# An attention kernel that feeds a mixture-of-experts layer: its start and the order of its stages and expert blocks were rearranged

## The chip, the cores and the metric

The kernel runs on one core of one Trainium2 chip. The metric is the device time of one execution in microseconds (us). The 13 executions of the kernel before lie within 0.24% of each other. For each kernel one execution was also profiled; its span, from the first to the last instruction, is about 2 us shorter than the time.

Ratios are the mean time of one kernel's runs over the mean time of the runs of the kernel before from the same rounds on the same chip. They are therefore not quite the ratios of the medians that are quoted beside them.

The engines are TensorE (PE in the profile, and PEld for its weight loads), VectorE (DVE), ScalarE (ACT), GpSimd (POOL, which here issues most DMAs) and SyncE (SP).

## The reference

Attention works on 4 batches of 8 heads. Each head has 768 positions in 8 blocks of 96 and a width of 64. A small 8 by 8 matrix per head goes through five Sinkhorn rounds and mixes the key blocks and value blocks. The attention output is a 3072 by 512 matrix x, which then goes through 8 experts, weighted by gates that take another eight Sinkhorn-like rounds.

```python
def _attn_ref(q, k, v, sort_net):
    # ... cut: shapes ...
    P = sort_net
    for _ in range(5):
        P = P - np.max(P, axis=-1, keepdims=True)
        P = np.exp(P)
        P = P / (np.sum(P, axis=-1, keepdims=True) + 1e-09)
        P = P / (np.sum(P, axis=-2, keepdims=True) + 1e-09)
    k_sorted = np.einsum('bhij,bhjcd->bhicd', P, k_b).reshape(B, H, S, D)
    v_sorted = np.einsum('bhij,bhjcd->bhicd', P, v_b).reshape(B, H, S, D)
    # ... cut: inside each block of 96: softmax(scale * q k_sorted^T) v_sorted ...

def _moe_ref(x, w_gate, w1, w2):
    P = np.exp(x @ w_gate - (x @ w_gate).max())
    for _ in range(8):
        P /= P.sum(1, keepdims=True) + 1e-09
        P /= P.sum(0, keepdims=True) + 1e-09
        P *= N / E
    for e in range(E):
        h = np.maximum(x @ w1[e], 0.0)
        out += P[:, e:e + 1] * (h @ w2[e])
```

## The kernel before

The kernel takes the heads in 16 pairs. A pair m goes through three stages. The first stage multiplies keys and values with a matrix R, built from the Sinkhorn result, and turns the queries with transposing matmuls. The second stage computes the scores, their exponents, and the turned values. The third, called the output stage below, computes the denominators, takes their reciprocals as Exp(-Ln), multiplies the exponents with the values, and writes into xtT, which holds x.

An expert block is a piece of `x @ w1[e]`: four matmuls of 128 by 512. It can run once the x of its batches is there. While attention goes on, such blocks fill TensorE between the stages. Before the first of them a pair takes 4.14 us (27.75 to 31.89 us), in which ScalarE is busy for 4.08 us, and its three stages need TensorE for only 2.69 us (1.0 + 0.98 + 0.71 us, by spacings near 45 us). Eleven of the 48 (expert, column) combinations, 88 blocks, are done this way, up to the point where the second layer starts.

The start: 36 matmuls on zeros ("spins") keep TensorE busy during the Sinkhorn rounds (10.86 of the first 13.20 us).

```python
    w_ = bank([128, 512])
    for _ in range(36):
        nc.tensor.matmul(w_, wide[:, 0:128], wide, start=True, stop=True)

    rs = ones.tile([32, 8], F32)
    Prep = carve([128, 8, 8, 16], BF16, 88 * KB)[0:32]
    Pt = P.rearrange("p i j -> p j i")
    nc.vector.reduce_max(out=rs, in_=P, axis=AX.X)
    nc.vector.tensor_sub(P, P, mkap(rs, [rs.ap[0], rs.ap[1], [0, 8]]))
    for it in range(5):
        nc.scalar.activation(out=P, in_=P, func=AF.Exp)
        nc.vector.reduce_sum(out=rs, in_=P, axis=AX.X)
        nc.vector.reciprocal(out=rs, in_=rs)
        nc.vector.tensor_tensor(out=P, in0=P, in1=mkap(rs, [rs.ap[0], rs.ap[1], [0, 8]]),
                                op=ALU.mult)
        nc.vector.reduce_sum(out=rs, in_=Pt, axis=AX.X)
        nc.vector.reciprocal(out=rs, in_=rs)
        if it < 4:
            nc.vector.tensor_tensor(out=Pt, in0=Pt, in1=mkap(rs, [rs.ap[0], rs.ap[1], [0, 8]]),
                                    op=ALU.mult)
        else:
            nc.vector.tensor_tensor(out=Prep, in0=mkap(P, [P.ap[0], [8, 8], [1, 8], [0, 16]]),
                                    in1=mkap(rs, [rs.ap[0], [0, 8], [1, 8], [0, 16]]), op=ALU.mult)
    pbp = bank([128, 8, 32])
    for i in range(8):
        nc.tensor.matmul(pbp[:, i, :], Prep[:, i].rearrange("g j c -> g (j c)"),
                         ident[0:32, 0:32], start=True, stop=True)
    Pbig = carve([128, 8, 32], F32, 90 * KB)
    nc.vector.tensor_copy(Pbig, pbp)
```

The stages. The kernel takes 8 buffers (banks) from PSUM, the memory that its matmuls write to, and `bank` hands them out in turn.

```python
    def stage1(m):
        kb, vb, qb = qkv[m]
        R = Rt[m]
        for src, dic, nm in ((kb, KT, "KT"), (vb, VT, "VT")):
            dic[m] = atp_.tile([128, 8, 6, 16], BF16, name=nm)
            for kh2 in range(2):
                b_ = bank([128, 3, 128])
                for k3 in range(3):
                    for h2 in range(2):
                        nc.tensor.matmul(b_[64 * h2:64 * h2 + 64, k3, :], src[:, h2, 3 * kh2 + k3, :],
                                         R[:, h2].rearrange("p i c -> p (i c)"), start=True, stop=True)
                dst = dic[m][:, :, 3 * kh2:3 * kh2 + 3, :].rearrange("d i kk c -> d kk i c")
                b_ = b_.rearrange("d kk (i c) -> d kk i c", c=16)
                if kh2 == 0 or (nm == "KT" and m > 5):
                    nc.scalar.copy(dst, b_)
                else:
                    nc.vector.tensor_copy(dst, b_)
        b_ = bank([128, 6, 128], BF16)
        for kk in range(6):
            for h2 in range(2):
                nc.tensor.matmul(b_[64 * h2:64 * h2 + 64, kk, :], qb[:, h2, kk, :], ident,
                                 is_transpose=True, start=True, stop=True)
        QT[m] = atp_.tile([128, 6, 128], BF16, name="QT")
        nc.vector.tensor_copy(QT[m], b_)
        if m + 1 < NPAIR:
            build_r(m + 1)

    def stage2(m):
        ATT[m] = [atp_.tile([96, 2, 384], BF16, name=f"at{h2}") for h2 in range(2)]
        for half in range(2):
            bb = [bank([96, 4, 96]) for _ in range(2)]
            for i4 in range(4):
                i = half * 4 + i4
                for h2 in range(2):
                    hs = slice(64 * h2, 64 * h2 + 64)
                    nc.tensor.matmul(bb[h2][:, i4, :], KT[m][hs, i].rearrange("d kk c -> d (kk c)"),
                                     QT[m][hs, :, 16 * i:16 * i + 16], start=True, stop=True)
            for h2 in range(2):
                nc.scalar.activation(out=ATT[m][h2][:, half, :], in_=bb[h2].rearrange("k i q -> k (i q)"),
                                     func=AF.Exp, scale=scale)
        b_ = bank([96, 8, 128], BF16)
        for i in range(8):
            nc.tensor.matmul(b_[:, i, :], VT[m][:, i].rearrange("d kk c -> d (kk c)"), ident, is_transpose=True,
                             start=True, stop=True)
        VS[m] = vs_[m % 2]
        nc.vector.tensor_copy(VS[m], b_.rearrange("c i (h d) -> c i h d", d=64))

    def stage3(m):
        b, hpi = m // 4, m % 4
        xo = xtT[:, hpi, b].rearrange("d kk (i c) -> d i kk c", c=16)
        for half in range(2):
            den = bank([128, 384])
            for h2 in range(2):
                nc.tensor.matmul(den[64 * h2:64 * h2 + 64, :], ones64[0:96], ATT[m][h2][:, half, :],
                                 start=True, stop=True)
            rc = atp_.tile([128, 384], F32, name="rc")
            nc.scalar.activation(out=rc, in_=den, func=AF.Ln)
            nc.scalar.activation(out=rc, in_=rc, func=AF.Exp, scale=-1.0)
            b_ = bank([128, 4, 96])
            for i4 in range(4):
                for h2 in range(2):
                    nc.tensor.matmul(b_[64 * h2:64 * h2 + 64, i4, :], VS[m][:, half * 4 + i4, h2, :],
                                     ATT[m][h2][:, half, 96 * i4:96 * i4 + 96], start=True, stop=True)
            nc.vector.tensor_tensor(out=xo[:, 4 * half:4 * half + 4],
                                    in0=b_.rearrange("d i (kk c) -> d i kk c", c=16),
                                    in1=rc.rearrange("d (i kk c) -> d i kk c", i=4, c=16), op=ALU.mult)
```

The order of stages and blocks:

```python
    def fill(n, both=True):
        for _ in range(n):
            if state["h"] >= len(blocks):
                return
            e, c, fb = blocks[state["h"]]
            if last_batch[c] > state["done"]:
                if state["m"] < 2:
                    spin(1)
                return
            h_block(e, c, fb, both)
            state["h"] += 1
    # ... cut ...
    build_r(0)
    for m in range(NPAIR + 3):
        state["m"] = m
        if m < NPAIR:
            stage1(m)
        if m + 4 < NPAIR:
            load_pair(m + 4)
        if m == 0:
            load_w1(0)
        if m == 5:
            load_w1(1)
        fill(1)
        if 1 <= m <= NPAIR:
            stage2(m - 1)
        fill(1)
        if 2 <= m <= NPAIR + 1:
            stage3(m - 2)
        fill(1)
        if m >= 6 and m % 4 == 2:
            gate(m // 4 - 1)
        fill(1)
        if m >= 5 and m % 4 == 1:
            state["done"] = m // 4 - 1
        if m in (11, 16):
            x_sums((m - 11) // 5)
```

The softmax here doesn't subtract the row's maximum and nothing guards it: scores larger than these inputs give would overflow.

## Time and profile before

| What | Before |
|---|---|
| Time, median of 13 runs | 678.72 us (678.14 to 679.74) |
| Span of the profiled execution | 676.4 us |
| First expert block starts (timeline) | 37.18 us |
| Second layer starts, after the last of the 88 blocks (timeline) | 151.95 us |
| From there to the end | 524.45 us |

The page's first part gives busy times, and its fourth part the shares of the chain of waits, the path of work that ended last. These are the lines for TensorE and for the chain by engine.

```profile
PE 665.0 (98%) x6508; PEld 546.2 (81%) x6534; DVE 541.2 (80%) x766; ACT 338.9 (50%) x640; POOL 121.7 (18%) x163
...
PE 93%; ACT 2%; POOL 1%; DMA 1%; issue 1%; DVE 1%; POOLq 0%; ACTq 0%
```

TensorE is the bottleneck nearly everywhere. A change can then help in three ways only: it gives TensorE less to do, it lets TensorE's useful work start sooner, or it removes gaps between pieces of that work.

The next view cuts the span into stretches. The columns are the stretch, its length, and the busy time and number of instructions of PE, PEld, DVE, ACT and POOL, then the granted TensorE clock (1.00 is full speed), the DMA share and GB/s.

```profile
0.00:13.20 13.20, 10.86 (x36) 4.15 (x36) 8.76 (x38) 2.77 (x7) 11.19 (x21) 1.00 0.93 126
13.20:20.25 7.05, 5.52 (x111) 3.98 (x112) 5.02 (x11) 3.02 (x8) 5.51 (x9) 1.00 1.39 199
20.25:37.18 16.93, 14.97 (x357) 12.53 (x357) 13.27 (x28) 16.32 (x41) 9.30 (x13) 1.00 1.26 204
...
152.11:676.40 524.29, 520.50 (x4733) 463.09 (x4734) 434.79 (x534) 228.39 (x398) 81.72 (x103) 1.00 0.47 85
```

PE's 10.86 us in the first stretch are spins, not work. From 20.25 to 37.18 us ScalarE is busy 16.32 of 16.93 us, and PE's 14.97 us there are stretched: the end of a matmul is modelled, so a busy PE is not a full PE. The work in it is read from the spacing of matmuls where TensorE runs without waits.

That is the third view: the timeline of TensorE over one pair that runs with expert blocks. The columns are start, length, engine, line, operation, output and inputs, the tile of the array that is used (rows * columns), the moving operand, and how many instructions were merged.

```profile
57.07 0.53 PE L183 MATMUL bank<-R,kb 128*64 128x128 bf16 x12
57.43 0.50 PE L183 MATMUL bank<-R,vb 128*64 128x128 bf16 x12
57.77 0.50 PE L194 MATMUL bank<-ident,qb 128*64 128x128 bf16 x12
58.20 1.04 PE L265 MATMUL bank<-xtT,w1r 128*128 128x512 bf16 x3
59.17 0.56 PE L209 MATMUL bank<-QT,KT 64*96 64x96 bf16 x16
59.66 0.65 PE L216 MATMUL bank<-ident,VT 128*96 128x128 bf16 x8
60.14 1.03 PE L265 MATMUL bank<-xtT,w1r 128*128 128x512 bf16 x4
61.10 0.35 PE L227 MATMUL bank<-at,ones 96*64 96x384 bf16 x2
61.29 0.34 PE L235 MATMUL bank<-at,bigf 96*64 96x96 bf16 x8
61.46 0.33 PE L227 MATMUL bank<-at,ones 96*64 96x384 bf16 x2
61.62 0.34 PE L235 MATMUL bank<-at,bigf 96*64 96x96 bf16 x8
61.89 1.90 PE L265 MATMUL bank<-xtT,w1r 128*128 128x512 bf16 x7
63.72 0.53 PE L183 MATMUL bank<-R,kb 128*64 128x128 bf16 x12
```

One pair takes 63.72 - 57.07 = 6.65 us. (Where a block shows three or seven matmuls instead of four or eight, a record is missing; the spacing shows that it ran.) A block streams in 4 x 0.216 = 0.86 us (the 12 matmuls from 127.11 us on take 2.59 us), but the single block at 60.14 is followed only 0.96 us later. Such gaps of about 0.1 us stand at several places of this pair.

### The profile page before, as it was taken

To read this page: it belongs to the slowest core of one execution; us is meant where nothing else is said; L and a number is where in the kernel's file an instruction comes from. 1 tells how busy PE (TensorE), PEld (TensorE's weight loads), DVE (VectorE), ACT (ScalarE), POOL (GpSimd) and SP (SyncE) were. 2 spreads that over 40 slices of the span, in tenths; PEclk is the share of its full clock that TensorE was granted. 3 is DMA by queue.
4 is the path that set the end of the run, shared out by engine and by line. 5 is a ranking of instruction groups with operands and counts; after the bars stand their busy time and mean duration, and the time that the engine had idled before them with its cause. 6 is when DMAs were issued, how large, how long until landed. Compare 5 with 4: busy or idle time off the path is not lost.

```text
span 676.4 us, 15404 instructions
## 1 busy us (share of the span) xinstructions
PE 665.0 (98%) x6508; PEld 546.2 (81%) x6534; DVE 541.2 (80%) x766; ACT 338.9 (50%) x640; POOL 121.7 (18%) x163
## 2 busy tenths in 40 slices
PE   7899999999999999999999999999999999999997
PEld 3765565448788888888888888888888888888886
DVE  6767666789899888987888997787698998677776
ACT  2888887662323444444544444444444454445441
POOL 8543000000212120121122032022012012102201
PEclk9999999999999999999999999999999999999999
DMA  9998108032365729551355678154075045235336
GB/s 141 204 205 119 24 2 126 0 71 66 113 160 120 162 82 181 82 79 16 64 79 92 112 115 134 35 79 62 17 124 96 2 78 78 28 53 79 43 83 125
DMA packets 45940, 59.77 MB, mean 88 GB/s; under 512 B 3760, under 2 KB 31408, under 8 KB 45744
## 3 DMA queue, kind: packets, MB, share of 16 engines
q0 software_dynamic: 37840, 50.35, 46.1%
q1 hardware_dynamic: 7616, 8.05, 4.1%
q8 instruction: 51, 0.84, 0.5%
q10 hardware_dynamic: 416, 0.39, 0.2%
q14 instruction: 17, 0.14, 0.1%
HBM read 59.79 MB, written 25.21 MB: 126 GB/s over the span
## 4 chain that ended last, share of the span: by engine, by line
PE 93%; ACT 2%; POOL 1%; DMA 1%; issue 1%; DVE 1%; POOLq 0%; ACTq 0%
PE a L515 25%; PE a L437 19%; PE g L515 12%; PE bank L265 11%; PE g L437 9%; PE b L515 6%; PE b L437 5%; PE bank L183 1%; DMA qb<-in_q_dram 1%; ACT at L212 1%; PE a L468 1%; PE bank L216 1%; PE bank L209 1%; PE bank L227 1%; ACT rc L230 1%
## 5 line engine op out<-in xcount | busy, mean ns | idle before, releaser
L515 PEld LDWEIGHTS <-bigf 128*128 128x128 bf16 x1520 | 148.7, 98 | 18.3
L524 POOL DMA_DIRECT2D out_dram<-bigf x92 | 72.4, 903 | 421.4 <-DVE bigf L534 397.4
L437 PEld LDWEIGHTS <-bigf 128*128 128x128 bf16 x1248 | 122.1, 98 | 14.1
L515 PEld LDWEIGHTS <-hS 128*128 128x128 bf16 x1152 | 112.6, 98 | 14.0 <-DVE hS L491 0.2
L477 DVE TENSOR_TENSOR bigf<-bigf 128x2048 bf16<-128x2048 bf16 x96 | 115.3, 1217 | 0.0
L442 ACT COPY bigf<-a 128x512 f32<-128x512 f32 x72 | 42.3, 587 | 114.9 <-PE a L437 107.9
L415 DVE CUSTOM_DVE_ANT_0 bigf<-g,bigf 128x512 bf16<-128x512 f32 x72 | 49.6, 689 | 51.5 <-ACT bigf L451 51.4
L437 PE MATMUL g<-xtT,bigf 128*128 128x256 bf16 x576 | 86.4, 273 | 0.0
L265 PE MATMUL bank<-xtT,w1r 128*128 128x512 bf16 x330 | 82.3, 379 | 1.6 <-DVE xtT L237 0.3
L437 PEld LDWEIGHTS <-w1r 128*128 128x128 bf16 x768 | 75.1, 98 | 8.7
L459 ACT ACTIVATE bigf<-a 128x512 bf16<-128x512 f32 x72 | 43.0, 597 | 44.0 <-PE a L437 44.0
L415 DVE CUSTOM_DVE_ANT_0 bigf<-b,bigf 128x512 bf16<-128x512 f32 x72 | 49.4, 687 | 19.3 <-ACT bigf L442 19.3
L265 PEld LDWEIGHTS <-w1r 128*128 128x128 bf16 x352 | 31.9, 99 | 32.7 <-issue 0.3
L447 ACT COPY bigf<-g 128x512 f32<-128x512 f32 x72 | 42.3, 587 | 23.2 <-PE g L437 23.1
L515 PE MATMUL a<-bigf 128*128 128x256 bf16 x384 | 52.9, 273 | 0.0
L451 ACT COPY bigf<-a 128x512 f32<-128x512 f32 x72 | 42.5, 590 | 20.2 <-PE a L437 19.1
L515 PE MATMUL a<-w2T,hS 128*128 128x256 bf16 x384 | 52.1, 273 | 0.0
L515 PE MATMUL g<-w2T,hS 128*128 128x256 bf16 x384 | 52.1, 273 | 0.0
L515 PE MATMUL a<-w2r,bigf 128*128 128x256 bf16 x384 | 50.9, 273 | 0.0
L415 DVE CUSTOM_DVE_ANT_0 bigf<-a,bigf 128x512 bf16<-128x512 f32 x72 | 49.3, 684 | 0.5 <-PE a L437 0.5
L515 PE MATMUL a<-w2T,bigf 128*128 128x256 bf16 x368 | 49.5, 273 | 0.0
L271 ACT ACTIVATE bigf<-bank 128x512 bf16<-128x512 f32 x62 | 37.1, 598 | 18.2 <-PE bank L265 16.7
(130 smaller groups left out, 986.9 us busy)
## 6 DMA issues: line engine op xcount, KB each, us to landing
out_dram<-bigf POOLq DMA_DIRECT2D x92, 256.0 KB, 5.3
w1r<-in_moe_w_dram POOLq DMA_DIRECT2D x6, 1024.0 KB, 10.7
bigf<-gdr SPq DMA_DIRECT2D x24, 256.0 KB, 6.5
bigf<-in_moe_w_dram POOLq DMA_DIRECT2D x6, 1024.0 KB, 14.6
w2r<-in_moe_w_dram POOLq DMA_DIRECT2D x4, 1024.0 KB, 12.3
kb<-in_k_dram POOLq DMA_DIRECT2D x16, 192.0 KB, 7.4
vb<-in_v_dram POOLq DMA_DIRECT2D x16, 192.0 KB, 7.3
qb<-in_q_dram POOLq DMA_DIRECT2D x16, 192.0 KB, 7.3
```

The lines of the kernel that those rows point to most:

```text
L183: nc.tensor.matmul(b_[64 * h2:64 * h2 + 64, k3, :], src[:, h2, 3 * kh2 + k3, :], R[:, h2].rearrange("p i c -> p (i c)"), start=True, stop= ...
L265: nc.tensor.matmul(b_, w1t[e][:, kk, fb * 128:(fb + 1) * 128], xf[:, kk, c * 512:(c + 1) * 512], start=(kk == 0), stop=(kk == 3))
L271: nc.scalar.activation(out=hT[e, c][:, fb, :], in_=b_, func=AF.Relu)
L415: nc.vector._custom_dve(TENSOR_ADD_SAT, out=out, in0=a, in1=b, s0=3.4028234663852886e38, s1=0.0)
L437: nc.tensor.matmul(b_[:, i, :], A[:, kk, 128 * (2 * j + i):128 * (2 * j + i) + 128], Bm[:, kk, :], start=(first and i == 0 and kk == 0), s ...
L442: nc.scalar.copy(cP1, al)
L447: nc.scalar.copy(cP5, ga)
L451: nc.scalar.copy(cU2, al)
L459: nc.scalar.activation(out=h[:, 4 + 2 * j:6 + 2 * j, 0:256], in_=al, func=AF.Relu)
L477: nc.vector.tensor_tensor(out=h, in0=h, in1=mkap(g, [g.ap[0], [0, f1 - f0], [1, 512]]), op=ALU.mult)
L515: nc.tensor.matmul(b_[:, g, :], A[P_][i][:, j, 128 * g:128 * g + 128], Bm[P_][i][:, j, :], start=(first and i == 0 and g == 0 and j == 0), ...
L524: nc.gpsimd.dma_start(out=out[bb * S:(bb + 1) * S].rearrange("(p kk) d -> kk p d", kk=6)[kk], in_=o_[:, tt, :], accum_op=ALU.add if p else ...
```

## The change

The change has these intents:

1. Bring four pairs through all their stages before anything else, plus one first stage, and then start expert blocks.
2. Turn the queries of pairs 0 and 1 during the Sinkhorn rounds, and load them earlier.
3. Shorten the end of the Sinkhorn chain: split the last product over VectorE and ScalarE, and build the first R straight from PSUM.
4. In each pair, take Ln, Ln, Exp, Exp instead of Ln, Exp, Ln, Exp, keep the output product back until `x_out`, and share the copies anew.
5. From pair 4 on, run scores, blocks, output stage of the pair before, first stage of the next pair, blocks.

The core of the diff:

```diff
-    w_ = bank([128, 512])
-    for _ in range(36):
-        nc.tensor.matmul(w_, wide[:, 0:128], wide, start=True, stop=True)
-
+    def spin(n):
+        b_ = bank([128, 512])
+        for _ in range(n):
+            nc.tensor.matmul(b_, wide[:, 0:128], wide, start=True, stop=True)
+
+    KT, VT, QT, ATT, VS, Rt = {}, {}, {}, {}, {}, {}
+
+    def turn_q(m, eng):
+        qb = qkv[m][2]
+        b_ = bank([128, 6, 128], BF16)
+        for kk in range(6):
+            for h2 in range(2):
+                nc.tensor.matmul(b_[64 * h2:64 * h2 + 64, kk, :], qb[:, h2, kk, :], ident,
+                                 is_transpose=True, start=True, stop=True)
+        QT[m] = atp_.tile([128, 6, 128], BF16, name="QT")
+        if eng is None:
+            return b_
+        eng(QT[m], b_)
+
+    spin(14)
     rs = ones.tile([32, 8], F32)
     Prep = carve([128, 8, 8, 16], BF16, 88 * KB)[0:32]
     Pt = P.rearrange("p i j -> p j i")
@@ -138,6 +155,12 @@
     nc.vector.tensor_sub(P, P, mkap(rs, [rs.ap[0], rs.ap[1], [0, 8]]))
     for it in range(5):
         nc.scalar.activation(out=P, in_=P, func=AF.Exp)
+        if it == 3:
+            nc.scalar.copy(QT[0], turned)
+        if it in (2, 4):
+            turned = turn_q(it // 2 - 1, None)
+            if it == 2:
+                spin(10)
         nc.vector.reduce_sum(out=rs, in_=P, axis=AX.X)
         nc.vector.reciprocal(out=rs, in_=rs)
         nc.vector.tensor_tensor(out=P, in0=P, in1=mkap(rs, [rs.ap[0], rs.ap[1], [0, 8]]),
...
@@ -148,33 +171,41 @@
             nc.vector.tensor_tensor(out=Pt, in0=Pt, in1=mkap(rs, [rs.ap[0], rs.ap[1], [0, 8]]),
                                     op=ALU.mult)
         else:
-            nc.vector.tensor_tensor(out=Prep, in0=mkap(P, [P.ap[0], [8, 8], [1, 8], [0, 16]]),
-                                    in1=mkap(rs, [rs.ap[0], [0, 8], [1, 8], [0, 16]]), op=ALU.mult)
+            nc.vector.tensor_tensor(out=Pt[:, :, 4:8], in0=Pt[:, :, 4:8],
+                                    in1=mkap(rs, [rs.ap[0], rs.ap[1], [0, 4]]), op=ALU.mult)
+            nc.scalar.copy(Prep[:, 4:8], mkap(P, [P.ap[0], [8, 4], [1, 8], [0, 16]], off=32))
+            nc.scalar.copy(QT[1], turned)
+            nc.vector.tensor_tensor(out=Prep[:, 0:4], in0=mkap(P, [P.ap[0], [8, 4], [1, 8], [0, 16]]),
+                                    in1=mkap(rs, [rs.ap[0], [0, 4], [1, 8], [0, 16]]), op=ALU.mult)
     pbp = bank([128, 8, 32])
     for i in range(8):
         nc.tensor.matmul(pbp[:, i, :], Prep[:, i].rearrange("g j c -> g (j c)"),
                          ident[0:32, 0:32], start=True, stop=True)
-    Pbig = carve([128, 8, 32], F32, 90 * KB)
-    nc.vector.tensor_copy(Pbig, pbp)
-
-    KT, VT, QT, ATT, VS = {}, {}, {}, {}, {}
+    Pbig = carve([128, 8, 32], BF16, 90 * KB)
 
...
+    def build_r(m, src):
         R = Rt[m] = atp_.tile([128, 2, 8, 16], BF16, name="R")
         nc.vector.tensor_tensor(
             out=R,
-            in0=mkap(Pbig, [Pbig.ap[0], [1, 2], [32, 8], [0, 16]], off=2 * m),
+            in0=mkap(src, [src.ap[0], [1, 2], [32, 8], [0, 16]], off=2 * m),
             in1=mkap(mask, [mask.ap[0], [0, 2], [0, 8], [1, 16]]),
             op=ALU.mult)
 
...
-    def stage1(m):
+    def stage1(m, mid=None):
         kb, vb, qb = qkv[m]
         R = Rt[m]
-        for src, dic, nm in ((kb, KT, "KT"), (vb, VT, "VT")):
+        acts = () if m == 3 else (("KT", 0),) if m == 2 else (("KT", 0), ("VT", 0)) if m < 6 else (("KT", 0), ("KT", 1), ("VT", 0))
+        for src, dic, nm in ((kb, KT, "KT"), (qb, QT, "QT"), (vb, VT, "VT")):
+            if nm == "QT":
+                if m not in QT:
+                    turn_q(m, nc.vector.tensor_copy)
+                if mid:
+                    mid()
+                continue
             dic[m] = atp_.tile([128, 8, 6, 16], BF16, name=nm)
             for kh2 in range(2):
                 b_ = bank([128, 3, 128])
@@ -184,22 +215,15 @@
                                          R[:, h2].rearrange("p i c -> p (i c)"), start=True, stop=True)
                 dst = dic[m][:, :, 3 * kh2:3 * kh2 + 3, :].rearrange("d i kk c -> d kk i c")
                 b_ = b_.rearrange("d kk (i c) -> d kk i c", c=16)
-                if kh2 == 0 or (nm == "KT" and m > 5):
+                if (nm, kh2) in acts:
                     nc.scalar.copy(dst, b_)
                 else:
                     nc.vector.tensor_copy(dst, b_)
...
-        if m + 1 < NPAIR:
-            build_r(m + 1)
-
-    def stage2(m):
-        ATT[m] = [atp_.tile([96, 2, 384], BF16, name=f"at{h2}") for h2 in range(2)]
+        if m + 1 < NPAIR and m:
+            build_r(m + 1, Pbig)
+
+    def scores(m):
+        ATT[m] = at_[m % 3]
...
                                      func=AF.Exp, scale=scale)
+
+    def turn_v(m):
...
+    AV = {}
+
     def stage3(m):
-        b, hpi = m // 4, m % 4
-        xo = xtT[:, hpi, b].rearrange("d kk (i c) -> d i kk c", c=16)
+        rc = []
         for half in range(2):
             den = bank([128, 384])
             for h2 in range(2):
                 nc.tensor.matmul(den[64 * h2:64 * h2 + 64, :], ones64[0:96], ATT[m][h2][:, half, :],
                                  start=True, stop=True)
-            rc = atp_.tile([128, 384], F32, name="rc")
-            nc.scalar.activation(out=rc, in_=den, func=AF.Ln)
-            nc.scalar.activation(out=rc, in_=rc, func=AF.Exp, scale=-1.0)
+            rc.append(atp_.tile([128, 384], F32, name="rc", bufs=4))
+            nc.scalar.activation(out=rc[half], in_=den, func=AF.Ln)
+        AV[m] = []
+        for half in range(2):
+            nc.scalar.activation(out=rc[half], in_=rc[half], func=AF.Exp, scale=-1.0)
             b_ = bank([128, 4, 96])
             for i4 in range(4):
                 for h2 in range(2):
                     nc.tensor.matmul(b_[64 * h2:64 * h2 + 64, i4, :], VS[m][:, half * 4 + i4, h2, :],
                                      ATT[m][h2][:, half, 96 * i4:96 * i4 + 96], start=True, stop=True)
+            AV[m].append((b_, rc[half]))
+
+    def x_out(m):
+        b, hpi = m // 4, m % 4
+        xo = xtT[:, hpi, b].rearrange("d kk (i c) -> d i kk c", c=16)
+        for half in range(2):
+            b_, rc = AV[m][half]
...
     def fill(n, both=True):
         for _ in range(n):
             if state["h"] >= len(blocks):
                 return
             e, c, fb = blocks[state["h"]]
             if last_batch[c] > state["done"]:
-                if state["m"] < 2:
-                    spin(1)
                 return
             h_block(e, c, fb, both)
             state["h"] += 1
+
+    def fill_two():
+        bs = blocks[state["h"]:state["h"] + 2]
+        bk = []
+        for kks in (range(3), range(3, 4)):
+            for n, (e, c, fb) in enumerate(bs):
+                if kks[0] == 0:
+                    if fb == 0:
...
-    build_r(0)
-    for m in range(NPAIR + 3):
-        state["m"] = m
+    build_r(0, pbp)
+    nc.scalar.copy(Pbig, pbp)
+    build_r(1, Pbig)
+    load_w1(0)
+    stage1(0)
+    load_pair(4)
+    stage1(1)
+    load_pair(5)
+    load_w1(1)
+    scores(0)
+    turn_v(0)
+    stage1(2)
+    load_pair(6)
+    scores(1)
+    stage3(0)
+    turn_v(1)
+    stage1(3)
+    load_pair(7)
+    x_out(0)
+    scores(2)
+    turn_v(2)
+    stage3(1)
+    scores(3)
+    x_out(1)
+    turn_v(3)
+    stage3(2)
+    x_out(2)
+    stage3(3)
+    stage1(4, lambda: x_out(3))
+    load_pair(8)
+    state["done"] = 0
+    fill_two()
+    for m in range(4, NPAIR + 1):
         if m < NPAIR:
-            stage1(m)
-        if m + 4 < NPAIR:
-            load_pair(m + 4)
-        if m == 0:
-            load_w1(0)
-        if m == 5:
-            load_w1(1)
-        fill(1)
-        if 1 <= m <= NPAIR:
-            stage2(m - 1)
-        fill(1)
-        if 2 <= m <= NPAIR + 1:
-            stage3(m - 2)
-        fill(1)
-        if m >= 6 and m % 4 == 2:
+            scores(m)
+            turn_v(m)
+        fill(1 if m < 8 else 2)
+        if m > 4:
+            stage3(m - 1)
+            x_out(m - 1)
+            if m % 4 == 0:
+                state["done"] = m // 4 - 1
+        if m + 1 < NPAIR:
+            stage1(m + 1)
+        if m + 5 < NPAIR:
+            load_pair(m + 5)
+        if m == 8:
+            fill_two()
+        else:
+            fill(2)
+        if m % 4 == 0:
             gate(m // 4 - 1)
-        fill(1)
-        if m >= 5 and m % 4 == 1:
-            state["done"] = m // 4 - 1
-        if m in (11, 16):
-            x_sums((m - 11) // 5)
-
+        if m in (9, 14):
+            x_sums((m - 9) // 5)
```

## The prediction

> **What bounds the kernel now.** TensorE. The page's first part has PE busy 665.0 of 676.4 us, and the chain of waits is 93% PE. From 152.1 us on (view by stretches) PE is busy 520.5 of 524.3 us, in code that the change leaves alone. What is left is the start. Until the first expert block, at 37.18 us in the timeline, PE does useful work for about 13.7 us only: six first stages at 1.0 us, five score stages at 0.98 and four output stages at 0.71 (spacings read near 45 us). The other 23.5 us are spin matmuls (36 at first, 10.9 us) and waits: for the Sinkhorn chain until 13.2 us, then for copies. From 20.25 to 37.18 us ScalarE is busy 16.3 of 16.9 us, and pairs come every 4.14 us, which is ScalarE's work for one.
>
> **What the change does.**
> 1. Expert blocks start after four pairs plus one first stage, not after six first stages and five score stages. That is the main gain.
> 2. Queries 0 and 1 are turned during the Sinkhorn, in idle PE and ScalarE time; 12 of 36 spin matmuls go.
> 3. The last Sinkhorn product (1.21 us on VectorE) becomes a small multiply and two halves on two engines, and the first R is built straight from PSUM, without the 0.43 us copy in front. Estimate: first useful pair at 13.8 instead of 14.57 us.
> 4. Ln, Ln, Exp, Exp replaces Ln, Exp, Ln, Exp, where each Exp waited for its Ln; some copies move to VectorE. With R's operands in bf16 its 0.42 us may shrink: [...] this trace agrees (512 bf16 elements of the x sums take 0.42 us, as 256 fp32 elements of R do). [...] I count on little.
> 5. Later, three blocks for a pair until pair 8, then four: 50 instead of 52 blocks are done when attention ends. The total of useful matmuls is unchanged.
>
> **Sum.** I laid the new order out, each engine in order, bank by bank, with the trace's durations; the same for the old order gives 37.3 us for the first expert block (trace: 37.2). The new one gives 29.4 us, with 11.8 us of useful work before it: waste 17.6 against 23.5 us, gain 5.9. Some 1.5 us go back: waits of 0.2 to 0.6 us for QT copies and banks in pairs 4 to 12, where scores follow their copies closely. Net 4.4 us, all on the critical path, since everything behind only shifts.
>
> Predicted: 674.3 us, 8 in 10 between 672.3 and 676.8. Faster by over 2% 0.01, within 2% 0.98, slower by over 2% 0.01.
>
> **What would show it.** In the timeline, first kb matmul near 13.8 and first expert block near 29.4 us; last attention-phase block near 147.7 instead of 152.1; the rest (524 us) unchanged within 0.5; ScalarE over 90% busy from 20 to 29 us; short waits of score matmuls for QT.
>
> **What would make it wrong.** The array's clock: now the first spins are 0.43 us apart until 7.2 us, 0.21 after (timeline). [...] with fewer spins and pauses of 2.5 us the array may slow again [...]. Late query loads could hold the Sinkhorn's Exp behind a QT copy. An unforeseen bank wait in the four-pair start, or late expert weights, would cost more.

Four passages are cut from it where the marks stand: what this case's traces do not show about R in bf16 and about the clock, and an estimate of the clock's cost that does not say from which numbers it comes. The sum: 5.9 - 1.5 = 4.4 us, and 678.7 - 4.4 = 674.3 us.

## The result

The changed kernel takes 672.55 us (median of 7 runs, 671.84 to 673.51), against 678.72 us before. The ratio is 0.9907, with a 95% interval of 0.9896 to 0.9917. The change is a gain of 0.9%, clear of noise. All outputs are right.

| What (profiled execution) | Before | Predicted | After |
|---|---|---|---|
| Time, median | 678.72 | 674.3 (672.3 to 676.8) | 672.55 |
| First matmul on keys | 14.57 | 13.8 | 13.69 |
| First expert block | 37.18 | 29.4 | 30.43 |
| Second layer starts | 151.95 | 147.7 | 146.36 |
| From there to the end | 524.45 | 524 | 524.44 |
| Span | 676.4 | | 670.8 |

The page of the kernel after, its first and fourth part:

```profile
PE 658.9 (98%) x6491; PEld 545.1 (81%) x6514; DVE 539.1 (80%) x766; ACT 337.2 (50%) x642; POOL 121.7 (18%) x163
...
PE 95%; DVE 3%; issue 1%; DMA 0%; ACT 0%
```

TensorE is still the bottleneck. The shares hardly move, because a gap that goes away at 98% busy is a small part of a long span. The whole gain lies before the second layer: behind it the two kernels take the same 524.4 us.

The stretches of the kernel after:

```profile
13.20:20.25 7.05, 6.39 (x135) 5.45 (x137) 5.50 (x12) 5.44 (x14) 5.04 (x7) 0.76 1.32 205
20.25:30.00 9.75, 8.68 (x193) 6.76 (x192) 7.98 (x18) 9.46 (x25) 4.28 (x6) 1.00 1.24 205
```

ScalarE is now busy 9.46 of 9.75 us from 20.25 to 30.00 us, so the four-pair start is still paced by it, as forecast. The clock column of the stretch from 13.20 us shows 0.76, where it showed 1.00 before.

One pair with four blocks in the kernel after, in the timeline of TensorE:

```profile
61.68 0.56 PE L233 MATMUL bank<-QT,KT 64*96 64x96 bf16 x16
62.17 0.65 PE L242 MATMUL bank<-ident,VT 128*96 128x128 bf16 x8
62.65 1.89 PE L301 MATMUL bank<-xtT,w1r 128*128 128x512 bf16 x7
64.47 0.52 PE L254 MATMUL bank<-bigf,ones 96*64 96x384 bf16 x4
64.82 0.51 PE L264 MATMUL bank<-bigf 96*64 96x96 bf16 x16
65.16 0.50 PE L214 MATMUL bank<-R,kb 128*64 128x128 bf16 x12
65.50 0.50 PE L143 MATMUL bank<-ident,qb 128*64 128x128 bf16 x12
65.83 0.50 PE L214 MATMUL bank<-R,vb 128*64 128x128 bf16 x12
66.27 1.90 PE L301 MATMUL bank<-xtT,w1r 128*128 128x512 bf16 x7
68.10 0.56 PE L233 MATMUL bank<-QT,KT 64*96 64x96 bf16 x16
```

The pair takes 68.10 - 61.68 = 6.42 us for the same matmuls as the 6.65 us before.

So three questions are open. What does the slow clock cost? Why is a pair 0.22 us shorter, where the prediction expected waits and a loss? And how much do the order and the new start bring, each by itself?

### The profile page after: what moved, and what is told of

Its sections match the earlier page's. It is cut to its first block, busy times and chain, and to the rows that moved or that the text cites. A ratio compares the mean times of both kernels' runs of the same rounds, so it can differ in the third digit from the quotient of the medians.

```text
span 670.8 us, 15351 instructions
## 1 busy us (share of the span) xinstructions
PE 658.9 (98%) x6491; PEld 545.1 (81%) x6514; DVE 539.1 (80%) x766; ACT 337.2 (50%) x642; POOL 121.7 (18%) x163
## 4 chain that ended last, share of the span: by engine, by line
PE 95%; DVE 3%; issue 1%; DMA 0%; ACT 0%
PE a L592 25%; PE a L514 19%; PE g L592 12%; PE bank L301 10%; PE g L514 9%; PE b L592 6%; PE b L514 5%; PE bank L214 1%; PE bank L242 1%; PE bank L233 1%; PE a L545 1%; PE bank L254 1%; PE bank L264 1%; PE bank L143 1%; PE bank L281 0%
## 5 line engine op out<-in xcount | busy, mean ns | idle before, releaser
L301 PE MATMUL bank<-xtT,w1r 128*128 128x512 bf16 x318 | 77.1, 379 | 1.0
## 6 DMA issues: line engine op xcount, KB each, us to landing
bigf<-in_moe_w_dram POOLq DMA_DIRECT2D x6, 1024.0 KB, 14.7
```

The costliest lines, as they stand in the source:

```text
L301: nc.tensor.matmul(b_, w1t[e][:, kk, fb * 128:(fb + 1) * 128], xf[:, kk, c * 512:(c + 1) * 512], start=(kk == 0), stop=(kk == 3))
```

## The experiments

This table collects the profiled executions. "Clock" is the mean granted clock over the span. In the kernel after a mean of 0.997 comes from about 3.4 us at a granted clock of 0.50 (14.4 to 17.8 us; 0.5 x 3.4 / 670.8 = 0.0025), so the column must be looked at before two rows are compared.

| Run | Clock | First block | Second layer starts | Span | Ratio to before (95%) |
|---|---|---|---|---|---|
| before | 1.000 | 37.18 | 151.95 | 676.4 | 1 |
| after | 0.997 | 30.43 | 146.36 | 670.8 | 0.9907 (0.9896 to 0.9917) |
| e1_warm | 1.000 | 29.22 | 145.16 | 669.6 | 0.9896 (0.9881 to 0.9911) |
| e2_order | 1.000 | 30.77 | 146.71 | 671.2 | 0.9917 (0.9904 to 0.9929) |
| e3_start | 0.997 | 34.39 | 149.17 | 675.8 | 0.9984 (0.9971 to 0.9996) |
| e4_ln_exp | 0.997 | 30.88 | 149.72 | 674.2 | 0.9954 (0.9942 to 0.9967) |
| e5_before_runs | 0.997 | 37.25 | 151.89 | 676.4 | 0.9982 (0.9969 to 0.9994) |
| e6_split | 0.997 | 30.44 | 146.20 | 670.7 | 0.9912 (0.9898 to 0.9925) |
| e7_gate_early | 1.000 | 33.65 | 148.39 | 672.9 | 0.9952 (0.9939 to 0.9966) |
| e8_one_run | 1.000 | 29.40 | 146.21 | 670.7 | 0.9910 (0.9896 to 0.9923) |
| e9_adjacent | 0.997 | 36.98 | 150.25 | 674.8 | 0.9954 (0.9941 to 0.9967) |
| e10_no_spin | 0.995 | 38.17 | 153.50 | 680.4 | 1.0039 (1.0022 to 1.0056) |
| e11_hole | 1.000 | 29.12 | 145.04 | 669.5 | 0.9895 (0.9882 to 0.9908) |

### The clock: e1_warm and e10_no_spin

The first experiment adds six spins to the changed kernel, in the hole of TensorE behind the second turn of queries.

```diff
-            if it == 2:
-                spin(10)
+            spin(10 if it == 2 else 6)
```

> The changed kernel with six more spin matmuls after the second query turn (about 11.1 to 12.4 us). Theory A (clock): the granted clock fell to 0.50 from about 14.3 to 17.6 us because TensorE was nearly idle from 11.05 to 13.7 us; filling that hole keeps 1.00, stages of pairs 0 and 1 run at full rate, first expert block comes 0.6 to 1.2 us earlier (29.3 to 29.8 instead of 30.43) and the time is 671.4 to 672.0 us. Rival B: that stretch waits for copies on VectorE and ScalarE anyway, so the clock is 1.00 but the time stays at 672.5 within 0.3.

These are single microseconds of the kernel after, in the view by stretches:

```profile
15.00:16.00 1.00, 1.00 (x22) 0.90 (x18) 0.90 (x2) 0.62 (x2) 0.72 (x1) 0.50 1.31 201
17.00:18.00 1.00, 1.00 (x12) 0.87 (x14) 0.09 (x2) 1.00 (x4) 0.76 (x2) 0.60 1.47 206
```

And these are the same two microseconds with the six spins:

```profile
15.00:16.00 1.00, 1.00 (x34) 0.85 (x29) 1.00 (x3) 1.00 (x3) 0.60 (x1) 1.00 1.29 198
17.00:18.00 1.00, 1.00 (x40) 0.91 (x35) 0.83 (x3) 0.74 (x2) 0.96 (x2) 1.00 1.21 213
```

The clock holds 1.00, and TensorE issues 34 instead of 22 and 40 instead of 12 matmuls in these two microseconds. The first expert block comes at 29.22 instead of 30.43 us, and the second layer starts 1.20 us earlier. Theory A holds: the pairs at the start did lose to the clock. The time is 671.97 us (median). That the gain is 1.2 us between two profiled executions does not make it 1.2 us on average: of the eight executions of the kernel after, two had a mean clock of 1.000 and spans of 670.0 us, and six had 0.995 or 0.997 and 670.5 to 671.6 us. The four executions with the spins all had 1.000 and spans of 669.6 to 670.2 us. The two ratios overlap, so the gain in time is likely but not clear of noise. That the spins hold the clock is clearer: all 12 executions with them (e1_warm, e8_one_run, e11_hole) had 0.999 or 1.000, and of the 17 executions of the new start and new order without them (the kernel after, e4_ln_exp, e6_split) only three had.

The kernel before has the same lottery. Of the nine executions measured beside this experiment, three had a mean clock of 0.999 or 1.000 and spans of 676.2 to 676.3 us; six had 0.995 or 0.997 and 677.4 to 677.7 us. Compared at full clock the change takes off 676.3 - 670.0 = 6.3 us; at 0.997 it takes off 677.4 - 670.8 = 6.6 us. So the clock blurs both kernels by about 1 us, and it is not the cause of the difference between them.

What makes the clock fall is not shown. In the kernel after it is 0.50 for about 3.4 us, from 14.4 to 17.8 us. TensorE was not empty before that: in the 3.4 us from 10.90 to 14.30 us, just before the drop, it counts as busy for 1.32 us. Nor does this number alone decide: e2_order was busy for only 0.80 us from 11.20 to 14.60 us and kept 1.00.

The other experiment goes the other way. It removes from the kernel before the seven spins that stand between the stages of pairs 0 and 1.

```diff
             if last_batch[c] > state["done"]:
-                if state["m"] < 2:
-                    spin(1)
                 return
```

> The kernel before without the seven spin matmuls between the stages of pairs 0 and 1 (they are not in the changed kernel either). Theory L (they stood on the chain: 0.8 us of the first pairs): first expert block 0.6 to 1 us earlier than 37.18, time down by 0.5 to 0.8 us where the clock stays 1.00. Rival M (they filled waits, and without them the clock falls to 0.50 more often): no gain or a loss, more executions with mean clock 0.997.

The time is 681.72 us, 0.4% slower than before, and all six executions have a mean clock between 0.994 and 0.997. In the profiled one the clock is at 0.50 for longer:

```profile
15.00:16.00 1.00, 1.00 (x24) 0.50 1.33 204
...
20.00:21.00 1.00, 1.00 (x17) 0.50 1.16 218
```

(This is the same view with TensorE alone: busy time and count, clock, DMA share, GB/s.) The first expert block comes 1.0 us later than before. Rival M is right about the outcome: without these useless matmuls the kernel is slower. Its mechanism is shown only in part. The clock fell at about 14.3 us, before the first of the removed spins would have run (15.92 us in the kernel before), so their absence did not start the slow stretch; it can only have made it last, here to about 21 us. And of the 4.0 us of span lost, 2.5 us are lost behind the second layer's start, where 526.9 instead of 524.45 us are spent; that is the wait of the next section.

### The order and the start, each alone: e2_order, e3_start, e7_gate_early

The second experiment keeps the new order and takes the start back (R in bf16 and the earlier loads of queries stay). "Order" here takes in all of intents 1, 4 and 5, so the copies and the order of Ln and Exp too.

```diff
-    spin(14)
+    spin(36)
-        if it == 3:
-            nc.scalar.copy(QT[0], turned)
-        if it in (2, 4):
-            turned = turn_q(it // 2 - 1, None)
... (the last Sinkhorn product as before, in one piece on VectorE)
-    build_r(0, pbp)
-    nc.scalar.copy(Pbig, pbp)
+    nc.vector.tensor_copy(Pbig, pbp)
+    build_r(0, Pbig)
```

> The new order of stages and blocks, but with the start as before: 36 spins, last Sinkhorn product whole on VectorE, copy of P to SBUF on VectorE before the first R, queries 0 and 1 turned in their first stage. Theory C (order is the main gain): about 674 us (673.3 to 674.8), first expert block near 31 us, so about 4.5 of the 6.2 us stay. Theory D (the early start is the main gain): 676 us or more.

It takes 673.19 us, ratio 0.9917. The order by itself brings most of the gain; theory C holds, and the value is at the better end of its range. Against e1_warm, which has the same order and also a full clock, the old start costs 30.77 - 29.22 = 1.55 us at the first block and 1.6 us of span. So the new start is worth 1.6 us in the new order when the clock holds, and 0.4 us in the profiled execution of the kernel after, where the clock fell.

The third experiment puts the new start into the old order of stages and blocks.

```diff
-    stage1(0)
-    load_pair(4)
... (the new sequence up to the end of the new loop)
+    for m in range(NPAIR + 3):
+        if m < NPAIR:
+            stage1(m)
... (the loop of the kernel before; stage2 is scores and turn_v, the output stage is followed by x_out;
     old copies, old order of Ln and Exp, no spins between the pairs)
```

> The new start (early query turns, split last product, first R from PSUM, bf16 R, no spins between pairs) in the old order of stages and blocks, old copies, old Ln and Exp order. Laid out with the durations of the trace: first expert block near 34 instead of 37.2 us and 675.5 us in all (674.8 to 676.5). Theory C strictly (only the order counts): 678 us, 0.8 us gained. If the clock falls as in the changed kernel, up to 1 us more.

The first block comes at 34.39 us and the second layer starts at 149.17 us, 2.8 us before the old one, although the clock fell to one half from about 13.0 to 16.4 us. But the time is 678.17 us, ratio 0.9984. The layout for this run was right up to the second layer, and the time was not. The span behind it is 526.6 instead of 524.45 us. The waits of TensorE from 140 us to the end name the place (columns: who waited for whom, us in total, times, longest):

```profile
PE a L564 <- DVE hS L540: 1.5, 1, 1.5
```

And the waits of VectorE between 100 and 160 us show what it waited for:

```profile
DVE bigf L526 <- DMA bigf<-gdr: 2.5, 1, 2.5
```

The final gates are written to DRAM and read back, spread over all partitions, before VectorE can multiply the experts' h with them and form the sums hS for the second layer. In the kernel before VectorE is busy with other sums from 142.93 to 147.81 us and goes on to this product at 147.85 us without a wait. The timelines show the issue of the first read and of the next expert's weights, and the start of VectorE's multiplication; first the kernel before, then e3_start:

```profile
144.54 0.90 SPq L403 DMA_DIRECT2D bigf<-gdr  x2
145.51 0.75 POOL L112 DMA_DIRECT2D w1r<-in_moe_w_dram  x1 [43.10 <-PE bank L265]
147.85 4.63 DVE L477 TENSOR_TENSOR bigf<-bigf 128x2048 bf16<-128x2048 bf16 x4
```

```profile
142.74 0.75 POOL L113 DMA_DIRECT2D w1r<-in_moe_w_dram  x1 [43.12 <-PE bank L299]
142.79 0.90 SPq L452 DMA_DIRECT2D bigf<-gdr  x2
147.59 3.50 DVE L526 TENSOR_TENSOR bigf<-bigf 128x2048 bf16<-128x2048 bf16 x3 [2.53 <-DMA bigf<-gdr]
```

In e3_start the 1 MB of weights was issued 0.05 us ahead of the gates, and VectorE starts at 147.59 us, 4.8 us after the read's issue. In the kernel before the gates went first, and VectorE starts without a wait 3.3 us after the issue. No run changed the order of these two DMAs alone, so that the weights slow the gates is not proven; but all 13 traces line up with it. In the eleven in which the read (256 KB) was issued 0.97 to 1.71 us ahead of the weights, VectorE started 3.2 to 3.7 us after the read's issue (in two of them, the kernel before and e5_before_runs, it waited for nothing, so the data may have landed sooner). In the two in which it came behind them it took longer: 4.8 us in e3_start, and 5.5 us in e10_no_spin, where it came 0.23 us behind. The weights' place explains only part of the wait in e3_start: there the read was issued 2.6 us after the write of the gates, against 1.6 us in the kernel before, and no run shows why. The kernel after has this wait of VectorE too (1.6 us), but it has 13 instead of 11 blocks left after the gate rounds, and TensorE does not notice (none of its waits from 140 us on names hS).

The seventh experiment tests that. It is e3_start with two blocks moved from pair step 16 to behind attention, so that the last gate stands 1.7 us earlier against the blocks. (With that the read of the gates also comes 1.1 us ahead of the weights, so both things change at once.)

```diff
             x_out(m - 2)
-        fill(1)
+        if m != 16:
+            fill(1)
         if m >= 6 and m % 4 == 2:
             gate(m // 4 - 1)
-        fill(1)
+        if m != 16:
+            fill(1)
```

> The earlier run of the new start in the old order, with two expert blocks moved from pair step 16 to behind attention, so that the last gate comes 1.7 us earlier against the blocks (13 blocks left after the gate iterations instead of 11, as in the changed kernel). Theory I (the new start alone gained 2.8 us by the phase's end, and the gates' round trip through DRAM gave most of it back): the wait of the second layer for VectorE sums (1.5 us) is gone and the time is 1 to 2 us less than that run, 676 to 677. Rival J (the loss of that run is not this wait): the same 678 within 0.4.

It takes 675.63 us, ratio 0.9952. TensorE no longer waits for hS, and 672.9 - 148.39 = 524.5 us are spent behind the start of the second layer. At a mean clock of 0.996 or 0.997 its executions have spans of 673.5 to 673.9 us, against 675.4 to 676.6 us for e3_start. Theory I holds: the new start alone is worth about 3.3 us, and without these two blocks it gives two thirds of that back.

The order alone is worth 5.6 us and the start alone 3.3 us (0.83% and 0.48% of 678.7 us). Together they bring 6.3 us, not 8.9. They overlap, because both shorten the stretch before the first expert block: in the profiled executions at full clock it comes 6.4 us earlier with the order alone (e2_order), 3.5 us with the start alone (e7_gate_early) and 8.0 us with both (e1_warm).

### The 0.22 us of a pair: e5_before_runs, e6_split, e8_one_run, e9_adjacent

The first guess was that each run of expert blocks between other matmuls costs a gap. Three experiments change the number of runs. The fifth merges blocks in the kernel before, with the changed kernel's order inside the output stage:

```diff
-        fill(1)
+        fill(2 if m > 5 else 1)
         if 1 <= m <= NPAIR:
             stage2(m - 1)
-        fill(1)
+        if m < 6:
+            fill(1)
... (output stage: den, den, av, av and Ln, Ln, Exp, Exp)
```

> The kernel before with only the order inside a pair changed: from pair 6 on its four expert blocks stand in two runs instead of three, and the output stage goes den, den, av, av with Ln, Ln, Exp, Exp. Theory G (each change between blocks and attention matmuls costs TensorE about 0.1 us): the distance of pairs falls from 6.64 to about 6.42 us, phase end 2 to 3 us earlier, time 675.6 to 677 us if the gates' round trip does not take some of it back. Rival H (the 0.22 us came from the order of pairs and lost waits, not from switches): 6.6 us and 678 us or more.

The sixth parts the two blocks of the changed kernel in pairs 9 to 15:

```diff
             scores(m)
+            if m > 8:
+                fill(1)
             turn_v(m)
-        fill(1 if m < 8 else 2)
+        fill(2 if m in (8, 16) else 1)
```

> The changed kernel with the two blocks before the output stage parted, one ahead of the value turn, one behind it, in pairs 9 to 15: one more switch each way in seven pairs, no copy waited for sooner. Theory G: the distance of those pairs grows from 6.42 to 6.5 to 6.62 us and the time by 0.6 to 1.4 us, to about 673.5. Rival H: nothing changes within 0.3 us.

The eighth puts all four blocks of a pair into one run, on top of e1_warm:

```diff
-        fill(1 if m < 8 else 2)
+        fill(1 if m < 8 else 2 if m == 8 else 0)
...
-            fill(2)
+            fill(2 if m < 8 else 4)
```

> The changed kernel with the six spins of the first experiment and all four blocks of pairs 9 to 15 in one run. Theory G: another 0.1 us per pair, 0.7 us in all, and the QT wait near 72 us gone: 671.0 to 671.5. Rival: waits for exponents and banks, since output and first stage now follow the scores at once: 672 or more.

Theory G fell in all three. With fewer runs in the old order a pair still takes 63.54 - 56.89 = 6.65 us. (The time is 677.47 us, ratio 0.9982; four of its five executions had a full clock and spans of 675.2 to 675.7 us, so about 0.8 us were gained, most likely in the early pairs, which come every 3.84 instead of 4.14 us near 30 us; none of it comes from the later distance.) With one more run in the new order a pair takes 71.54 - 65.15 = 6.39 us, a little less than 6.42, and the time is the same (672.76 us). With one run the time is 672.73 us, 0.8 us more than e1_warm, and a pair takes 75.62 - 68.92 = 6.70 us.

The timelines hold the answer: the gaps stand where the column with the asterisk, the tile of the array, changes its kind. Here is a part of e5_before_runs:

```profile
60.34 0.65 PE L216 MATMUL bank<-ident,VT 128*96 128x128 bf16 x8
60.92 0.52 PE L228 MATMUL bank<-at,ones 96*64 96x384 bf16 x4
61.27 0.51 PE L237 MATMUL bank<-at,bigf 96*64 96x96 bf16 x16
61.71 1.90 PE L269 MATMUL bank<-xtT,w1r 128*128 128x512 bf16 x8
63.54 0.53 PE L183 MATMUL bank<-R,kb 128*64 128x128 bf16 x12
```

The value turn (128*96) takes 0.48 us where a block follows it, as at 62.17 us of the kernel after, and 0.58 us here, where the output stage (96*64) follows. The output stage takes 0.34 us for its second half where the first stage (128*64) follows, as at 64.82 us of the kernel after, and 0.44 us here, where a block (128*128) follows. Between two tiles of the same width of 64 columns there is no gap (the 0.34 us above), nor between a value turn and a block (the 0.48 us). Going by the tiles, a pair passes six changes in the old order: 64 columns (first stage), full (block), 64 rows (scores), full (turn, block), 64 columns (output), full (block), and again 64 columns. In the new order output stage and next first stage stand side by side, and four changes remain. Merging or parting blocks, as e5_before_runs and e6_split do, changes neither count, and neither does e8_one_run. Of its 0.28 us more, 0.17 us stand at the key matmuls (68.92 to 69.43 us: 0.51 instead of 0.34 us); where the rest comes from was not tracked down.

So the guess is now that a change of the tile's kind (theory K below calls it the tile mode) is what costs the time. The ninth experiment puts this to the test in the old order of pairs: from pair 6 on the output stage moves next to the following first stage, and its blocks stand ahead of it.

```diff
         fill(1)
+        fill(1 if m > 5 else 0)
         if 1 <= m <= NPAIR:
             stage2(m - 1)
         fill(1)
-        if 2 <= m <= NPAIR + 1:
-            stage3(m - 2)
-        fill(1)
         if m >= 6 and m % 4 == 2:
             gate(m // 4 - 1)
-        fill(1)
+        fill(1 if m > 5 else 0)
+        if 2 <= m <= NPAIR + 1:
+            stage3(m - 2)
+        fill(0 if m > 5 else 2)
... (output stage: den, den, av, av and Ln, Ln, Exp, Exp, as in e5_before_runs)
```

> The kernel before with den, den, av, av and, from pair 6 on, the output stage directly ahead of the next first stage (its block moved ahead of it; three runs of blocks became two). Theory K (what costs about 0.1 us is a change of tile mode of the array: full, 64 columns or 64 rows; the old order has six such changes a pair, the earlier run with merged runs still had six and gained nothing, the changed kernel has four): four changes, distance of pairs 6.42 to 6.45 us, phase end 1.5 to 2.3 us before 151.95. Rival H (the 0.22 us came from lost waits that only the new order of pairs removes): 6.6 us or more. The time itself may hide part of it where the gates' round trip binds: 676 to 677.5 us.

A pair now takes 61.70 - 55.28 = 6.42 us:

```profile
55.28 0.52 PE L228 MATMUL bank<-at,ones 96*64 96x384 bf16 x4
55.63 0.51 PE L237 MATMUL bank<-at,bigf 96*64 96x96 bf16 x16
55.97 0.50 PE L183 MATMUL bank<-R,kb 128*64 128x128 bf16 x12
...
61.70 0.52 PE L228 MATMUL bank<-at,ones 96*64 96x384 bf16 x4
```

The second layer starts at 150.25 us and the time is 675.81 us, ratio 0.9954. The same kernel order with six changes (e5_before_runs) has 0.9982. Theory K holds: two changes of the tile's kind fewer go with 0.22 us less for each pair (6.65 to 6.42 us), an estimate of about 0.11 us each, and this needs neither the new order of pairs nor the new start. What the change from the 64-row scores to a full-array matmul costs cannot be read here: such a matmul follows them in every order, and they take 0.49 us. The groups of weight loads show it from another side. These are the loads ahead of the key matmuls from 37 to 118 us (after the bar: idle time of the loader just before them, and what ended it). First the kernel before:

```profile
L183 PEld LDWEIGHTS <-kb 128*64 128x64 bf16 x108 | 3.3, 109 | 3.8 <-issue 3.8
```

Then the kernel after:

```profile
L214 PEld LDWEIGHTS <-kb 128*64 128x64 bf16 x120 | 3.8, 110 | 0.0
```

Before, the weight loader sat idle 0.42 us ahead of each of the nine groups of key matmuls in that stretch (9 x 0.42 = 3.8 us), and the first weights of the new kind were loaded only when their matmuls began (both at 63.72 us). After, the kind does not change there, and it does not sit idle; e9_adjacent, in the old order of pairs, shows 0.0 there too.

### The order of Ln and Exp: e4_ln_exp

The fourth experiment takes back Ln, Ln, Exp, Exp in the changed kernel.

```diff
         for half in range(2):
             den = bank([128, 384])
... (two matmuls)
             nc.scalar.activation(out=rc, in_=den, func=AF.Ln)
-        for half in range(2):
             nc.scalar.activation(out=rc, in_=rc, func=AF.Exp, scale=-1.0)
             b_ = bank([128, 4, 96])
... (the output matmuls)
```

> The changed kernel with Ln, Exp, Ln, Exp for a pair again, and den, av, den, av on TensorE. Theory E (the pairing matters because the output product of a pair stands ahead of the next pair's query copy on VectorE): waits of about 0.5 us at blocks or scores in most pairs, 675 to 676 us. Rival F (ScalarE is off the critical path after the start, [...]): 673 to 674 us.

(From rival F a clause is cut, a cost of tile changes for each pair that no run shows; it was the author's reason for 0.5 to 1.5 us over the 672.55 us of the changed kernel.)

It takes 676.09 us, ratio 0.9954: 3.5 us are lost, half of the gain. The size is theory E's, but its mechanism is not. The waits of TensorE from 13.2 us on name a copy of queries only once, for 0.3 us before the first block; in the pairs they name the Ln:

```profile
PE bank L299 <- ACT rc L257: 1.5, 7, 0.2
PE bank L214 <- ACT rc L257: 0.8, 2, 0.6
```

The second Ln stands behind the first Exp on ScalarE, which itself waits for the first Ln, so the second bank of denominators comes free later, and the block (L299) or the next key matmul (L214) that is to use this bank waits. The pairs with four blocks take 6.7 us, for example 79.67 - 72.94 = 6.73 us. In most of them a wait of 0.21 us for the Ln makes up most of the 0.26 us by which they are longer (6.68 instead of 6.42 us); the rest was not tracked down. In the old order the same change of Ln and Exp left the pair at 6.65 us (e5_before_runs), so this loss belongs to the new order.

### Two instructions moved into pauses of VectorE: e11_hole

In the fourth Sinkhorn round VectorE runs two small instructions for later use in front of a product. The eleventh experiment is e1_warm with these moved into VectorE's pauses during an Exp.

```diff
-    nc.vector.tensor_copy(identh, ident)
...
+            if it == 2:
+                nc.vector.tensor_copy(identh, ident)
+            if it == 3:
+                with nc.allow_low_precision("one nonzero term"):
+                    nc.vector.reduce_sum(out=mask, in_=ident.rearrange("p (j c) -> p c j", c=16), axis=AX.X)
```

> The first experiment (six more spins) and the cast of the fp16 identity and the sum for the mask moved into VectorE's pauses while ScalarE computes an Exp of the Sinkhorn, instead of in front of a product of its fourth round. The trace shows that round 0.33 us longer than the others. Expected: first kb matmul at 13.2 to 13.3 instead of 13.6 us, phase end 0.3 us earlier, time 671.5 to 671.7, against 671.97. Rival: the pauses are too short and nothing changes.

The first key matmul comes at 13.34 instead of 13.59 us, but the first block only 0.10 us and the second layer 0.12 us earlier. The time is 672.06 us, ratio 0.9895, the same as e1_warm within noise. The expectation of 0.3 us was too high. e1_warm and e11_hole have the lowest ratios of all, and both beat the kernel before; that they beat the changed kernel is likely from their spans, and not clear of noise.

## Why the prediction was right or wrong

The time lay inside the range, 1.75 us below the forecast value. The steps:

- **The bottleneck: right.** PE stays at 98%, and behind the second layer's start 524.45 and 524.44 us are spent.
- **The earlier first block: right in mechanism, 1.0 us off.** 29.4 us was forecast and 30.43 measured. The layout itself was good: with the clock held, e1_warm has 29.22 us. What it missed is the clock, and the prediction had named that danger ("with fewer spins and pauses of 2.5 us the array may slow again") without putting it into the sum. It cost 1.2 us in the profiled execution. The account of the kernel before, however, is off by one stage: not six but seven first stages run before its first block (their key matmuls start at 14.57, 17.09, 20.25, 23.23, 27.75, 31.89 and 36.02 us). So the useful work before 37.18 us is about 14.7 us, the waste 22.5 us, and the gain laid out for the first block 4.9 instead of 5.9 us. The forecast of 147.7 us then leaves 0.5 us that go back, not 1.5.
- **The earlier first pair: right.** 13.69 against 13.8 us.
- **"Some 1.5 us go back": wrong, and this is the term that was mis-sized.** From the first block to the second layer before took 151.95 - 37.18 = 114.77 us, and after took 146.36 - 30.43 = 115.93 us. After has 14.7 - 11.8 = 2.9 us more of useful work to do in it (two first stages and one score stage). So 2.9 - 1.16 = 1.7 us were gained there, where 1.5 us (0.5 with the right count) were to be lost. The profile names one wait for a query copy, 0.3 us at 23.39 us, ahead of the first block; from the first block on it names one wait of 0.2 us, and a gap of 0.3 us stands before the query turn at 72.23 us. What the prediction did not have was the changes of the tile's kind: four instead of six, 0.22 us a pair (e9_adjacent shows it in the old order). Ten output stages of the kernel after stand next to a first stage, which makes an estimate of 2.2 us; less the gap of 0.3 us this is close to the 1.7 us. The sum put the cost of a pair at its work and its waits alone.
- **bf16 for R: rightly left at little.** R's instruction takes 0.41 to 0.43 us with bf16 inputs, as it did with fp32 inputs (0.42 us).
- **ScalarE over 90% busy from 20 to 29 us: right**, 97% from 20.25 to 30.00 us.

The two misses, +1.0 us up to the first block and -2.4 us from there (115.93 us instead of 147.7 - 29.4 = 118.3 us), add to the -1.3 us by which the second layer started earlier than forecast. That they have opposite signs is luck, and so is that the time came out this close.

## What to carry to other kernels

When TensorE is the bottleneck, read the gaps between its groups against the tile of the array that each group uses, and place groups of the same kind of tile side by side; here two changes of kind fewer went with 0.22 us less a pair (e9_adjacent), and merging blocks without removing a change left a pair at 6.65 us (e5_before_runs). Fill the holes of the start with matmuls on zeros, but check the granted clock over several executions: with six more of them it stayed full in all 12, and removing seven went with 0.4% more time, though more than half of that (2.5 of 4.0 us in the profiled execution) came by way of the gates. When work is pulled forward, ask which chain was hidden behind it: the new start alone lost two thirds of its gain to the gates' way through DRAM, until two blocks were left behind to cover it.
